# Routed experts behind a short convolution: the head laid out in a written order, with chunk 2's convolution inside

## The chip, the cores and the metric

The kernel runs on one core of a Trainium2 chip. The metric is the device time of one execution in microseconds: the median of three runs is 1276.24 us (1272.69 to 1276.6). Engines are called as in the profile: PE (TensorE matmul), PEld (its weight loads), DVE (VectorE), ACT (ScalarE), POOL (GpSimd), SP (SyncE, which only issues transfers here).

## The reference

The input x has 8 sequences of 3584 tokens with 192 channels, in fp32. Two stages are computed, one after the other:

```python
# 1. causal convolution: 8 heads of 24 channels, 7 taps, softmax of the taps
out = np.einsum('hk,bskhg->bshg', w, x_unf)
# 2. routing to one of 8 experts by cosine similarity, 1024 hidden channels
logits = (x/|x|) @ (emb/|emb|).T / tau
expert_idx = np.argmax(logits, axis=1); gate_w = softmax(logits)[expert_idx]
h = np.maximum(x[mask] @ w1[e], 0.0)
out[mask] = gate_w[mask, None] * (h @ w2[e])
```

There are 28672 tokens. Each expert has w1 (192 x 1024) and w2 (1024 x 192) in fp32, 1.5 MB together.

## The kernel before, in words

The tokens are cut into 16 chunks of 1792 (16 tiles of 112 tokens). For a chunk, `load_x` fetches its tokens into one of two buffers. `mix` does the convolution: for each of 8 heads a PE matmul in fp32 with a banded matrix (`band`, L377; two matmul records per head), an ACT copy out of PSUM (L380), then the squared norms of the tiles (L389 on ACT for 12 tiles, L392 on DVE for 4), powers of two and an inverse norm from a chain of small DVE operations (`rsqrt`, L140 to L143, then L401 to L405). `route` scales the tokens (L424 on DVE), makes fp16 high parts (L426 on ACT) and low parts (L428, L431 on DVE) in a buffer `rows` (two of them, by the chunk's parity), turns them so that channels lie on partitions, and multiplies by the experts (`logits`, L557). The rest of `route` is the ranking: softmax, the best expert, and a running count that gives every token a place `di` (L471 to L527) in a table `rows_d` in DRAM, sorted by expert. Sixteen indirect transfers per chunk, issued by POOL (L573), scatter the rows there.

An expert block is 256, 512 or 1024 tokens of one expert. `fetch` brings its rows back transposed (`e_xT`, L700, a transfer on SP's queue that waits for the scatters that it needs), `expert` does the two matmuls (L745 and L768, in split fp16), with ACT and DVE moving the hidden layer (L749, L751), and POOL scatters the result (L775). The block's expert is known only on the chip; DVE copies its weights from the image `res` into `slot` (L677, L679, L680, L683).

The experts' weights are used as fp16 high and low parts. `prep_load` brings one expert's raw weights, three transfers; `prep_weights` takes the sum of squares (a PE product, L306, whose diagonal DVE sums, L311), a power of two (L316, L151, L157, L319), three ACT operations for the high parts (L325) and three DVE operations for the low parts (L329). For experts 3 to 7 the sum of squares of w2 is an ACT operation instead (L297). Raw weights have three places: `hid`, `slot` and the end of `res`.

The head is what runs before the first expert block: constants, all eight experts' weights, chunks 0 and 1 convolved, routed and scattered. In the head the turning is done by PE (L459) with ACT copies (L463); later by transfers on SP's queue (`xtb<-rows`, 16 per chunk, L569). After chunk 1, `hand_out(2)` chooses the first seven blocks of 256 (`select`), and later hand-outs come after chunks 3, 5, 8 and 12.

What sets the order: SP's queue is in the order of the program. The other engines' queues are laid out by a scheduler in the framework with its own estimate of times; edges without a semaphore (`_dep(..., False)`) hold one instruction behind another on an engine. In the head, `HEAD` says how many steps of the chunks' work follow each step of an expert's weights, and `BEHIND` holds the work of experts 3 to 7 behind chunk 1's. After the head, `PRE` steps of the chunks' work are written ahead of the first block:

```python
PRE = 56
BEHIND = 3
HEAD = 9, 8, 9, 0, 0, 0, 0, 0
```

Then each step of a block releases some steps of the chunks' work (`dispatch`), with `TURN` steps held between the turning and the logits of a chunk.

Of the kernel before, what the change touches and what calls it, by code (L numbers as in the profile page):

```python
# [26 lines left out]
E = 8  # L27
# [42 lines left out]
class _Moe:  # L70
    def __init__(self, ctx, tc, x, weight, emb, tau, w1, w2, out):
# [35 lines left out]
        self.weights_in, self.later = False, []  # L107
# [54 lines left out]
    def constants(self):  # L162
# [20 lines left out]
        tmp = self.op.tile([128, D], F32, tag="y", name="tmp")[:, 0:2 * E].bitcast(I32)  # L183
# [9 lines left out]
        cbi = tmp[:, E:]  # L193
# [7 lines left out]
    def conv_taps(self, w):  # L201
# [19 lines left out]
        st = [self.prep_load(0)]  # L221
# [5 lines left out]
        st.append(self.prep_load(1))  # L227
        self.load_x(1)
        return st + [self.prep_load(2)]
# [54 lines left out]

    def prep_weights(self, e, st):
        nc = self.nc
# [5 lines left out]
        for k, cols in enumerate(  # L292
                ([(128, i) for i in range(NFC)] + [(64, i) for i in range(NFC, 2 * NFC)],
                 [(128, i) for i in range(2 * NFC, 2 * NFC + NFC * D // 128)])):
            if k and e >= BEHIND:

                i = nc.scalar.activation(  # L297
                    out=img[:, W2:W2 + NFC * D], in_=st[:, 2 * F:], func=AF.Square,
                    accum_out=acc[:, k:k + 1]).ins
                _dep(self.tc, i, self.act.name, False)  # L300
                yield
                continue
            tr = self.ps("h", [128, 128], F32, "tr_ps")
            for n, (rows, i) in enumerate(cols):
                v = sr[0:rows, i * 128:(i + 1) * 128]
                i = nc.tensor.matmul(out=tr, lhsT=v, rhs=v, start=(n == 0),  # L306
                                     stop=(n == len(cols) - 1)).ins
                if e >= BEHIND:
                    _dep(self.tc, i, self.turned.name, False)
            dg = self.sp.tile([128, D], F32, tag="sq", name="w_dg")[:, 0:128]  # L310
# [14 lines left out]
        hi = [nc.scalar.activation(out=o, in_=i, func=AF.Copy, scale=m).ins  # L325
              for o, i, m in ((img[:, 0:F], st[:, 0:F], s1),
                              (xb[0:64, :], st[0:64, F:2 * F], s1[0:64]),
                              (b[:, :, 0:D], s_b, s2))]
        lo = [nc.vector.scalar_tensor_tensor(  # L329
            out=o, in0=i, scalar=m, in1=h, op0=ALU.mult, op1=ALU.subtract).ins  # L330
              for o, i, m, h in (
                  (img[:, F:2 * F], st[:, 0:F], s1, img[:, 0:F]),
                  (xb[64:128, :], st[0:64, F:2 * F], s1[0:64], xb[0:64, :]),
                  (b[:, :, D:], s_b, s2, b[:, :, 0:D]))]
        self.split = lo[0]
        if e >= BEHIND:
            for i in hi:
                _dep(self.tc, i, self.act.name, False)
            for i in lo:
                _dep(self.tc, i, self.dve.name, False)  # L340
        elif e:
            for i in lo:
                _dep(self.tc, i, self.cut.name, False)
        yield


    def load_x(self, c):
# [4 lines left out]
        lo, ld = 0, []  # L352
        if r0 == 0:
            nc.gpsimd.memset(xt[0:HALO, 0, :], 0.0)
            ld = [nc.sync.dma_start(out=xt[HALO:128, 0, :], in_=xb[0:TP, :]).ins]
# [5 lines left out]
        ld.append(nc.sync.dma_start(out=xt[:, lo:, :], in_=src).ins)  # L361

        if c in self.later:
            for i in ld:
                _dep(self.tc, i, self.split.name)
# [4 lines left out]
    def mix(self, c, ring, first):  # L370
# [15 lines left out]
        for t in range(NT):  # L386
            sq = sp.tile([128, D], F32, tag="sq", name="sq")[0:TP, :]
            if t % 4 < NACT:
# [9 lines left out]
        s, si = self.pow2(n2[:], [TP, NT], 195, "x_p")  # L398
        y = self.rsqrt(n2[:], [TP, NT], "x_r")
# [7 lines left out]

        yield 1.5, 0.0
        self.mixed[c] = xc, s, si, f


    def route(self, c, xbar):
        xTs = []
        nc, sp = self.nc, self.sp
        xc, s, si, f = self.mixed.pop(c)
        r32 = self.rows2[:, c % 2]
        rows = r32.bitcast(F16)
        lg = self.ps("l", [128, NT, 2 * E], F32, "lg_ps")
        nc.vector.tensor_single_scalar(out=r32[:, :, D], in_=self.ids,
                                       scalar=float(c * CT), op=ALU.add)  # L420
        for g in range(0, NT, GX):
            u = slice(g, g + GX)
            sb = s[:, u].unsqueeze(2).to_broadcast([TP, GX, D])
            nc.vector.tensor_tensor(out=xc[:, u, :], in0=xc[:, u, :], in1=sb,  # L424
                                    op=ALU.mult)
            nc.scalar.copy(out=rows[:, u, 0:D], in_=xc[:, u, :])  # L426
            yield 0.9, 0.85
            nc.vector.tensor_tensor(  # L428
                out=rows[:, u, 256:384], in0=xc[:, u, 0:128],
                in1=rows[:, u, 0:128], op=ALU.subtract)  # L430
            self.cut = nc.vector.tensor_tensor(  # L431
                out=rows[:, u, 192:256], in0=xc[:, u, 128:192],
                in1=rows[:, u, 128:192], op=ALU.subtract).ins
            yield 0.95, 0.0

            if xbar and g < 2 * GX:
                xTs.append(self.turn(rows, g, GX))
        if c + 2 < self.nch:
            if self.weights_in:
                self.load_x(c + 2)  # L440
            else:
                self.later.append(c + 2)
        if xbar:
            for g in range(2 * GX, NT, GX):
                xTs.append(self.turn(rows, g, GX))
        if xbar:
            yield self.clock + TURN
            for g in range(NT // GX):
                self.logits(lg, xTs, g)
                yield 0.2, 0.2  # L450
                yield self.clock + GAP
        else:
            for g in range(NT // GX):
                xT = self.xt_next()
                xv = xT[:, 0:XW].rearrange("p (a k t) -> p a k t", k=3, t=TP)
                for k in range(3):
                    tp = self.ps("r", [128, GX, TP], F16, "tr_ps")
                    for a in range(GX):
                        self.turned = nc.tensor.transpose(  # L459
                            out=tp[:, a, :],  # L460
                            in_=rows[:, g * GX + a, k * 128:(k + 1) * 128],
                            identity=self.idh[:TP, :TP]).ins
                    nc.scalar.copy(out=xv[:, :, k, :], in_=tp)  # L463
                    yield 0.0, 0.5
# [419 lines left out]
    def run(self):  # L884
# [25 lines left out]
        for _ in a:  # L910
            pass
# [58 lines left out]
```

## Time and profile before

| what | value |
|---|---|
| median of the runs | 1276.24 us |
| the profiled execution: its own time, and its span | 1276.24 us, 1274.5 us |
| PE, DVE, ACT, POOL busy over the span | 89%, 66%, 46%, 43% |
| first scatter of chunk 0 starts, last scatter of chunk 1 ends | 71.68 us, 115.72 us |
| first matmul of the first block starts | 124.58 us |

The profile's times start at the beginning of the span. Busy time of an engine is the time in which at least one of its instructions ran; a row of a timeline gives start, duration, engine, line, operation, and in brackets how long the engine stood idle before it and what ended that.

### The profile page before, as it was taken

The numbers are of one execution on the slowest core, as the hardware profiler recorded it, in microseconds if no ns is written. First come the engines' busy times: TensorE is split into PE (matmuls) and PEld (weight loads), VectorE is DVE, ScalarE is ACT, GpSimd is POOL, SyncE is SP. The second block draws the span as 40 slices with busy tenths as digits, with TensorE's granted clock in tenths as the row PEclk, the third lists the DMA queues.
The fourth block names the chain that finished last, engine by engine and source line by source line (L and its number), as shares of the span: only waits on it lengthen the run. The fifth ranks groups of instructions, "written<-read, shape, count | busy, mean of one in ns | idle before, by whom it ended". The sixth has DMA issues, their size and how long they took to land.

```text
span 1274.5 us, 31268 instructions
## 1 busy us (share of the span) xinstructions
PE 1135.3 (89%) x10560; PEld 879.3 (69%) x10560; DVE 836.3 (66%) x2193; ACT 584.5 (46%) x1345; POOL 548.8 (43%) x536
## 2 busy tenths in 40 slices
PE   5543887698999999999989999999999999999998
PEld 2432666587668777666887577756777777788797
DVE  3984687598658887568696656574446545477475
ACT  3963753344545545545545453333333434333332
POOL 0055017646555745555745456474222221232222
PEclk9655989898999999999999999999999999999999
DMA  9365255664755665654536435224211122112120
GB/s 262 100 194 160 38 133 133 163 141 93 152 131 119 148 144 117 148 135 106 147 84 158 102 77 121 62 76 88 53 39 49 42 57 40 44 37 57 39 48 18
DMA packets 273432, 129.25 MB, mean 101 GB/s; under 512 B 215246, under 2 KB 263757, under 8 KB 273280
## 3 DMA queue, kind: packets, MB, share of 16 engines
q1 hardware_dynamic: 249472, 80.39, 28.4%
q0 software_dynamic: 23808, 46.87, 13.2%
q8 instruction: 91, 1.49, 0.5%
q14 instruction: 61, 0.50, 0.1%
HBM read 38.35 MB, written 47.53 MB: 67 GB/s over the span
## 4 chain that ended last, share of the span: by engine, by line
PE 40%; DVE 3%; issue 3%; POOL 2%; DMA 2%; ACT 2%; POOLq 0%; DVEq 0%; ACTq 0%; SPq 0%
PE h_ps L745 20%; PE o_ps L768 19%; DMA rows_d<-rows,di 1%; POOL rows_d L573 1%; PE conv_ps L377 1%; DVE slot L683 1%; ACT hid L749 1%; POOL out_dram L775 1%; DVE hid L751 1%; ACT sq L389 1%; DVE slot L677 0%; DMA e_xT<-rows_d 0%; DVE xt L424 0%; DVE slot L680 0%; PE lg_ps L557 0%
## 5 line engine op out<-in xcount | busy, mean ns | idle before, releaser
L768 PE MATMUL o_ps<-slot,hid 128*128 128x192 f16 x5544 | 504.2, 248 | 28.1 <-DVE slot L683 11.3
L768 PEld LDWEIGHTS <-hid 128*128 128x128 f16 x5544 | 463.2, 98 | 69.4 <-issue 19.9
L775 POOL DMA_INDIRECT out_dram<-y,e_mt x231 | 258.4, 1119 | 485.9 <-ACT y L773 449.0
L751 DVE SCALAR_TENSOR_TENSOR hid<-h_ps,hid 128x512 f16<-128x512 f32 x462 | 313.7, 686 | 146.6 <-ACT hid L749 138.8
L749 ACT ACTIVATE hid<-h_ps 128x512 f16<-128x512 f32 x462 | 271.1, 596 | 274.8 <-PE h_ps L745 263.0
L745 PE MATMUL h_ps<-e_xT,slot 128*128 128x256 f16 (+2 forms) x2592 | 343.1, 271 | 24.7 <-DMA e_xT<-rows_d 17.5
L573 POOL DMA_INDIRECT rows_d<-rows,di x256 | 273.1, 1067 | 176.4 <-issue 57.6
L745 PEld LDWEIGHTS <-slot 128*128 128x128 f16 x2592 | 222.5, 100 | 89.3 <-issue 17.0
L745 PE MATMUL h_ps<-e_xT,res 128*128 128x512 f16 x1088 | 278.8, 379 | 5.8 <-DMA e_xT<-rows_d 2.7
L773 ACT ACTIVATE y<-o_ps,g 128x192 f32<-128x192 f32 x231 | 94.2, 419 | 222.6 <-PE o_ps L768 194.9
L745 PEld LDWEIGHTS <-res 128*128 x1088 | 104.5, 98 | 126.6 <-issue 11.1
L683 DVE COPY slot<-res 128x3074 f16 x88 | 85.5, 972 | 127.1 <-PE o_ps L768 125.6
L377 PE MATMUL conv_ps<-xt,band 128*112 128x384 f32 x256 | 109.9, 525 | 19.0 <-DMA xt<-in_dram 16.0
L426 ACT CAST rows<-xt 112x768 f16<-112x768 f32 x64 | 52.9, 832 | 97.1 <-DMA rows_d<-rows,di 53.4
L380 ACT COPY xt<-conv_ps 112x384 f32<-112x384 f32 x128 | 61.1, 480 | 54.1 <-PE conv_ps L377 52.3
L389 ACT ACTIVATE sq<-xt 112x192 f32<-112x192 f32 x192 | 67.9, 355 | 4.8 <-DVE sq L392 2.7
L377 PEld LDWEIGHTS conv_ps<-xt,band 128*112 128x112 f32 x256 | 41.6, 190 | 32.7 <-issue 22.4
L677 DVE COPY slot<-res 128x3072 f16 x58 | 56.3, 971 | 4.7 <-PE h_ps L745 3.2
L424 DVE TENSOR_TENSOR xt<-xt,x_p_s 112x768 f32<-112x768 f32 x64 | 58.2, 949 | 0.1
L428 DVE TENSOR_TENSOR rows<-xt,rows 112x512 f16<-112x512 f32 x64 | 43.8, 684 | 19.1 <-ACT rows L426 17.7
L557 PEld LDWEIGHTS <-xtb 128*128 128x128 f16 x768 | 29.0, 98 | 22.9 <-DMA xtb<-rows 11.6
L557 PE MATMUL lg_ps<-ma,xtb 128*128 128x16 f16 x512 | 30.9, 171 | 15.0 <-DMA xtb<-rows 9.8
(168 smaller groups left out, 594.3 us busy)
## 6 DMA issues: line engine op xcount, KB each, us to landing
xt<-in_dram SPq DMA_DIRECT2D x8, 1536.0 KB
xt<-in_dram SPq DMA_DIRECT2D x8, 1440.0 KB
rows_d<-rows,di POOLq DMA_INDIRECT x256
out_dram<-y,e_mt POOLq DMA_INDIRECT x231
xtb<-rows SPq DMA_TRANSPOSE x224
hid<-in_dram SPq DMA_DIRECT2D x3, 768.0 KB
slot<-in_dram SPq DMA_DIRECT2D x3, 768.0 KB
hid<-in_dram SPq DMA_DIRECT2D x3, 512.0 KB
```

Source lines behind the costliest of these rows:

```text
L377: self.behind(nc.tensor.matmul(out=ps, lhsT=self.band[:, h, :], rhs=xt[:, :, h * G:(h + 1) * G], start=True, stop=True))
L380: nc.scalar.copy(out=xc[:, :, h * G:(h + 1) * G], in_=ps)
L389: nc.scalar.activation(out=sq, in_=xc[:, t, :], func=AF.Square, accum_out=n2[:, t:t + 1])
L557: i = self.nc.tensor.matmul(out=lg[:, g * GX + a, :], lhsT=xTs[g][:, u:u + 128], rhs=self.mb if k == 1 else self.ma, start=(k == 0), stop= ...
L573: i = self.nc.gpsimd.indirect_dma_start(out=self.rows_d[:, :], out_offset=bass.IndirectOffsetOnAxis(ap=idx, axis=0), in_=src, in_offset=No ...
L683: self.nc.vector.tensor_copy(out=self.slot[:, S2:], in_=self.res[:, bass.ds(self.we + W2, RES - W2)])
L745: mm = nc.tensor.matmul(out=ps[:, c, :], lhsT=w1(o, b + c), rhs=xT[:, k, :], start=(i == 0), stop=(i == 4))
L749: self.step = nc.scalar.activation(out=hh[:, b:b + m, :], in_=ps, func=AF.Relu).ins
L751: nc.vector.scalar_tensor_tensor(out=hl[:, b:b + m, :], in0=ps, scalar=0.0, in1=hh[:, b:b + m, :], op0=ALU.max, op1=ALU.subtract)
L768: mm = nc.tensor.matmul(out=o, lhsT=h[:, c, q], rhs=w2[:, c, k:k + D], start=(c + i == 0), stop=(c == NFC - 1 and i == 2))
L773: self.step = nc.scalar.activation(out=y, in_=o, func=AF.Copy, scale=g[:, a:a + 1]).ins
L775: i = nc.gpsimd.indirect_dma_start(out=self.out[:, :], out_offset=bass.IndirectOffsetOnAxis(ap=mt[:, a, 0:1], axis=0), in_=y, in_offset=No ...
```

## The change

Up to the last split of the weights, PE, DVE and ACT get one written order: a string `HEAD` of 174 characters says whose next step follows. A digit is the next step of chunk 0, 1 or 2, a letter that of expert a to h's weights. Afterwards a loop ties each instruction of PE, DVE and ACT to the one before it on its engine with an edge without a semaphore.

A chunk's generator `first` has these steps: 1 to 8 the heads of the convolution, 9 to 16 two tiles of squared norms each, 17 the powers of two; then 18 scale group 0, 19 scale 1, 20 low parts of 0, 21 scale 2, 22 low 1, 23 scale 3, 24 and 25 turn, 26 low 2, 27 and 28 turn, 29 low 3, 30 the inverse norms (`factor`), 31 to 38 turn and logits, 39 to 41 the ranking up to `di`, 42 the scatters, and for chunk 1 43 the first hand-out. Chunk 2 has only steps 1 to 17, with its inverse norms in 17. An expert's generator has 9: two sums of squares, the power of two, three high parts, three low parts.

The loads on SP's queue are: chunk 0's tokens, the band, expert a's weights, chunk 1's tokens, experts b to e, and, as places come free, chunk 2, f, g, h and chunk 3. There are five places for raw weights: three at the end of `res`, `hid` and `slot`. The sum of squares of w2 is PE's for all experts. The numbers 0 to 63 of `select` become a constant. Behind the head, `dispatch` starts with chunk 2 mixed and chunk 3 to mix, and `PRE` goes from 56 to 39.

```diff
-PRE = 56
+PRE = 39
-BEHIND = 3
-HEAD = 9, 8, 9, 0, 0, 0, 0, 0
+RAW = 2 * (2 * F + F * D // 128)
+AREAS = (2, 0), (2, 2), (2, 1), (0, 0), (1, 0), (2, 0), (0, 0), (1, 0)
+HEAD = ("0000000000000a000a00aa01101a0a011a10101aa001b111b0110110001b0b1bb1bccb"
+        "00cc0ccb0c1cc1dde100101d01dd221de20ed1ee21dd112121ee1e1211e1211222221f"
+        "f2122ff2ffffggfhh0g11ggghhghghghhh")
@@ conv_taps
-        st = [self.prep_load(0)]
         self.band = cp.tile([128, H, TP], F32, name="band")
...
-        st.append(self.prep_load(1))
-        self.load_x(1)
-        return st + [self.prep_load(2)]
@@ prep_load
-        st = (self.hid[:], self.slot[:], self.res[:, (E - 2) * RES:])[e % 3].bitcast(F32)[:, 0:2 * F + NFC * D]
+        k, n = AREAS[e]
+        at = E * RES - (n + 1) * RAW if k == 2 else 0
+        st = (self.hid, self.slot, self.res)[k][:, at:at + RAW].bitcast(F32)
@@ prep_weights
-            if k and e >= BEHIND:
-                i = nc.scalar.activation(
-                    out=img[:, W2:W2 + NFC * D], in_=st[:, 2 * F:], func=AF.Square,
-                    accum_out=acc[:, k:k + 1]).ins
...
+        for o, i, m in ((img[:, 0:F], st[:, 0:F], s1),
+                        (xb[0:64, :], st[0:64, F:2 * F], s1[0:64]),
+                        (b[:, :, 0:D], s_b, s2)):
+            nc.scalar.activation(out=o, in_=i, func=AF.Copy, scale=m)
+            yield
...
@@ mix
-            sq = sp.tile([128, D], F32, tag="sq", name="sq")[0:TP, :]
+            sq = self.lp.tile([128, D], F32, tag="sqa" if act else "sqv", name="sq")[0:TP, :]
@@ new: first
+    def first(self, c):
+        nc = self.nc
+        yield from self.mix(c, "h")
+        if c >= PICK[0]:
+            return
+        rows = self.rows2[:, c % 2].bitcast(F16)
+        f = lg = None
+        steps = [(self.scaled, 0), (self.scaled, 1), (self.rest, 0), (self.scaled, 2),
+                 (self.rest, 1), (self.scaled, 3), 0, 1, (self.rest, 2), 2, 3,
+                 (self.rest, 3), None, 4, 5, 6, 7, 8, 9, 10, 11]
...
+        yield from self.rank(c, lg, f)
@@ dispatch
+        last, cb, ca = self.nch, PICK[0], PICK[0] + 1
@@ run
-        st = self.conv_taps(w)
+        self.conv_taps(w)
+        st = [self.prep_load(0)]
+        self.load_x(1)
+        st += [self.prep_load(e) for e in range(1, 5)]
         self.embeddings(em, tb)
...
+        work = {"012"[c]: self.first(c) for c in range(PICK[0] + 1)}
+        work.update({"abcdefgh"[e]: self.prep_weights(e, st) for e in range(E)})
+        load = lambda e: lambda: st.append(self.prep_load(e))
+        wait = [("0", 29, lambda: self.load_x(2)), ("a", 9, load(5)),
+                ("d", 9, load(6)), ("e", 9, load(7)), ("1", 29, lambda: self.load_x(3))]
+        done = dict.fromkeys(work, 0)
+        for k in HEAD:
+            next(work[k])
+            done[k] += 1
+            while wait and done[wait[0][0]] >= wait[0][1]:
+                wait.pop(0)[2]()
...
+        end = {}
+        for i in self.nc.cur_bb.bb.instructions[at:]:
+            if i.engine in (self.nc.tensor.engine, self.nc.vector.engine,
+                            self.nc.scalar.engine):
+                if i.engine in end:
+                    _dep(self.tc, i, end[i.engine].name, False)
+                end[i.engine] = i
+        self.mm = end[self.nc.tensor.engine].name
         while self.ready < min(3, len(self.subs)):
             self.fetch()
-        a = self.dispatch(first, "r")
+        a = self.dispatch()
```

The ranking (`rank`) and the halves of a group (`scaled`, `rest`, `factor`) are the code of `route` and `mix` before, cut into functions.

## Rows read from the trace of the kernel before

**Rows 1.** Busy us by stage (x instructions), granted PE clock, DMA share, GB/s

```profile
45.00:71.70 26.70, 15.00 (x196) 12.01 (x195) 24.85 (x82) 22.11 (x44) 0.06 (x2) 0.50 0.40 119
71.70:110.00 38.30, 10.67 (x79) 8.57 (x76) 30.04 (x87) 25.80 (x26) 30.07 (x28) 0.50 0.49 151
110.00:124.60 14.60, 5.67 (x11) 2.63 (x12) 3.38 (x5) 2.40 (x5) 5.87 (x6) 0.62 0.83 254
```

**Rows 2.** Timeline, end of the head: places, scatters, fetch, first block

```profile
71.68 1.10 POOL L573 DMA_INDIRECT rows_d<-rows,di  x1 [26.64 <-DVE di L527]
...
79.27 0.15 DVE L527 TENSOR_SCALAR di<-dr 112x16 int32<-112x16 f32 x1
79.32 0.94 POOL L573 DMA_INDIRECT rows_d<-rows,di  x1 [0.30 <-issue]
...
109.93 2.05 POOL L573 DMA_INDIRECT rows_d<-rows,di  x1 [0.31 <-issue]
110.91 0.95 DVE L677 COPY slot<-res 128x3072 f16 x1
...
114.78 0.94 POOL L573 DMA_INDIRECT rows_d<-rows,di  x1 [0.30 <-issue]
...
121.34 1.33 SPq L700 DMA_TRANSPOSE e_xT<-rows_d  x1
...
124.58 4.00 PE L745 MATMUL h_ps<-e_xT,slot 128*128 128x256 f16 x18 [3.40 <-DMA e_xT<-rows_d]
...
127.11 1.31 SPq L700 DMA_TRANSPOSE e_xT<-rows_d  x1
```

**Rows 3.** Timeline, begin of the head: the band's load and the first convolution

```profile
9.62 0.38 SPq L224 DMA_DIRECT2D band<-cseq_d  x1
...
16.63 7.54 PE L377 MATMUL conv_ps<-xt,band 128*112 128x384 f32 x16 [2.79 <-issue]
```

**Rows 4.** DVE by line and shape, 0 to 124 us: busy us, mean ns

```profile
L424 DVE TENSOR_TENSOR xt<-xt,x_p_s 112x768 f32<-112x768 f32 x8 | 7.3, 948 | 0.0
L329 DVE SCALAR_TENSOR_TENSOR res<-hid,w_p_s,res 128x1536 f16<-128x1536 f32 x3 | 5.4, 1811 | 0.0
L428 DVE TENSOR_TENSOR rows<-xt,rows 112x512 f16<-112x512 f32 x8 | 5.4, 679 | 0.0
L329 DVE SCALAR_TENSOR_TENSOR res<-hid,w_p_s,res 128x1024 f16<-128x1024 f32 x3 | 3.8, 1277 | 0.7 <-ACT res L325 0.7
L431 DVE TENSOR_TENSOR rows<-xt,rows 112x256 f16<-112x256 f32 x8 | 3.3, 412 | 0.0
L311 DVE SCALAR_TENSOR_TENSOR w_dg<-tr_ps,idf 128x128 f32<-128x128 f32 x11 | 3.1, 285 | 18.9 <-ACT sq L389 11.0 <-PE tr_ps L306 7.6
L141 DVE SCALAR_TENSOR_TENSOR x_r_t<-x_r_t,n 112x16 f32<-112x16 f32 x6 | 1.0, 170 | 0.1
```

**Rows 5.** Chain that ended last: one step, the landing of a scatter

```profile
611.77 2.46 DMA rows_d<-rows,di
```

**Rows 6.** PE by line, 124.5 to 150 us

```profile
L377 PE MATMUL conv_ps<-xt,band 128*112 128x384 f32 x22 | 9.7, 522 | 0.0
```

**Rows 7.** Waits of PE, 124 to 260 us: total, times, longest

```profile
PE h_ps L745 <- DMA e_xT<-rows_d: 17.5, 4, 10.6
PE lg_ps L557 <- DMA xtb<-rows: 9.8, 10, 2.1
```

**Rows 8.** Timeline after the head: chunk 2's turning, scatters, eighth fetch, a later wait

```profile
146.78 10.82 SPq L569 DMA_TRANSPOSE xtb<-rows  x8
...
158.74 13.10 SPq L569 DMA_TRANSPOSE xtb<-rows  x8
...
189.48 1.55 POOL L573 DMA_INDIRECT rows_d<-rows,di  x1 [15.40 <-DVE sl_ai L613]
...
218.84 2.41 SPq L700 DMA_TRANSPOSE e_xT<-rows_d  x1
...
251.51 2.31 PE L745 MATMUL h_ps<-e_xT,slot 128*128 128x256 f16 x10 [10.56 <-DMA e_xT<-rows_d]
```

More of the change, by code (lines that the diff above doesn't have):

```diff
@@ L191, in constants @@
         nc.gpsimd.memset(self.rst[:, :, 0:1], 0.0)
-        cbi = tmp[:, E:]
+        nums = tmp[0:1, E:E + 64]
+        nc.gpsimd.iota(nums, pattern=[[1, 64]], base=0, channel_multiplier=0)
+        self.nums = cp.tile([1, 64], F32, name="nums")
+        nc.vector.tensor_copy(out=self.nums, in_=nums)
+        cbi = tmp[:, E + 64:]
         nc.gpsimd.iota(cbi, pattern=[[self.cap, E]], base=0, channel_multiplier=0)
@@ L305, in prep_weights @@
                 v = sr[0:rows, i * 128:(i + 1) * 128]
[L306 to L310, printed above, removed]
+                nc.tensor.matmul(out=tr, lhsT=v, rhs=v, start=(n == 0),
+                                 stop=(n == len(cols) - 1))
+            dg = self.lp.tile([128, D], F32, tag="sqv", name="w_dg")[:, 0:128]
             nc.vector.scalar_tensor_tensor(
@@ L360, in load_x, with mix @@
             ap=[[D, 128], [TP * D, NT - lo], [1, D]])
[L361 to L365, printed above, removed]
+        nc.sync.dma_start(out=xt[:, lo:, :], in_=src)
         self.xts.append(xt)
-    def mix(self, c, ring, first):
+    def mix(self, c, ring):
         nc, sp = self.nc, self.sp
@@ L406, in mix @@
                                 scalar2=None, op0=ALU.mult)
-        yield 1.5, 0.0
-        self.mixed[c] = xc, s, si, f
-    def route(self, c, xbar):
-        xTs = []
-        nc, sp = self.nc, self.sp
[L415 to L464, printed above, removed]
-                xTs.append(xT)
-                self.logits(lg, xTs, g)
-                yield 0.2, 0.2
@@ new lines, in factor, with scaled, rest @@
+        return f
+    def scaled(self, c, g):
+        xc, s = self.mixed[c][:2]
+        u = slice(g * GX, g * GX + GX)
+        sb = s[:, u].unsqueeze(2).to_broadcast([TP, GX, D])
+        self.nc.vector.tensor_tensor(out=xc[:, u, :], in0=xc[:, u, :], in1=sb,
+                                     op=ALU.mult)
+        self.nc.scalar.copy(out=self.rows2[:, c % 2].bitcast(F16)[:, u, 0:D],
+                            in_=xc[:, u, :])
+    def rest(self, c, g):
+        xc, u = self.mixed[c][0], slice(g * GX, g * GX + GX)
+        rows = self.rows2[:, c % 2].bitcast(F16)
+        self.nc.vector.tensor_tensor(
+            out=rows[:, u, 256:384], in0=xc[:, u, 0:128],
+            in1=rows[:, u, 0:128], op=ALU.subtract)
+        self.nc.vector.tensor_tensor(
+            out=rows[:, u, 192:256], in0=xc[:, u, 128:192],
+            in1=rows[:, u, 128:192], op=ALU.subtract)
@@ new lines, in route @@
+    def route(self, c):
+        xTs = []
+        lg = self.ps("l", [128, NT, 2 * E], F32, "lg_ps")
+        for g in range(NT // GX):
+            self.scaled(c, g)
+            yield 0.9, 0.85
+            self.rest(c, g)
+            yield 0.95, 0.0
+            if g < 2:
+                xTs.append(self.turn(c, g))
+        if c + 2 < self.nch:
+            self.load_x(c + 2)
+        for g in range(2, NT // GX):
+            xTs.append(self.turn(c, g))
+        yield self.clock + TURN
+        for g in range(NT // GX):
+            self.logits(lg, xTs[g], g)
+            yield 0.2, 0.2
+            yield self.clock + GAP
+        yield from self.rank(c, lg, self.mixed[c][4])
@@ L479, in route @@
         ex = sp.tile([TP, NT, E], F32, tag="ea", name="ex")
-        self.act = nc.scalar.activation(out=ex, in_=l, func=AF.Exp).ins
+        nc.scalar.activation(out=ex, in_=l, func=AF.Exp)
+        if head:
+            yield
         z = sp.tile([TP, NT], F32, tag="z", name="z")
@@ L505, in route @@
         yield 2.5, 0.2
-        if xbar:
+        if not head:
             yield self.clock + RANK
@@ L533, in route @@
             self.hand_out(c + 1)
-        while self.pend and not xbar:
-            self.put()
-            yield 0.15, 0.15
+        if head:
+            while self.pend:
+                self.put()
+            yield
+        if c + 1 == PICK[0]:
+            self.hand_out(c + 1)
+            yield
     def put(self, step=None):
```

138 lines of the change are left out of this document (70 added, 68 removed).

## The prediction

> **What bounds the kernel now.** I read the page, then the stretches, then the timeline of the head's end, then the waits of PE behind it. Up to 110 us the head belongs to DVE: 24.85 of 26.7 us busy from 45 to 71.7, 30.04 of 38.3 from 71.7 to 110, while PE has 15.0 and 10.67 [rows 1]. From 110 to 124.6 nothing computes much (DVE 3.38, ACT 2.40 of 14.6). What ends last is a chain on POOL: the scatters start at 71.68, when chunk 0's places are ready, and end at 114.78 + 0.94 = 115.72, the first fetch is issued at 121.34, the first matmul of a block starts at 124.58 [rows 2]. So 32 scatters took 44.04 us, 1.376 each. Chunk 1's places came at 79.27 + 0.15 = 79.42 [rows 2], when POOL still had some ten scatters of chunk 0 to do, so they never made POOL wait.
>
> Behind the head PE does not simply run. From 124 to 260 us it waits 17.5 us for a block's rows and 9.8 for turned tokens [rows 7]. The reason is SP's queue: chunk 2 is loaded, convolved and cut late, so its turning starts at 146.78, and its 16 transfers hold the queue to 158.74 + 13.10 = 171.84, with the fetches of later blocks behind them; its scatters start at 189.48 and the eighth fetch, the first that needs them, is issued at 218.84 [rows 8]. One wait of 10.56 us stands later, at 251.51 [rows 8]. The profiled execution has the median's time, 1276.24 us, its span 1274.5; sums below are against it.
>
> **The change: begin of the head.** The band's load is issued at 9.62, after the taps have landed, and the first convolution starts at 16.63 and takes 7.54 [rows 3]. In the band's queue stood expert a's 1.5 MB; now only chunk 0's tokens do. At least nothing is won, at most the band lands as a scatter does, 2.46 us [rows 5] after 9.62 + 0.38, and the start moves by 16.63 - 12.46 = 4.2. I take 3.9, near the upper end, since what stood ahead is gone: start 12.7, end 20.2, copies and first DVE work at 21.2. Five places for raw weights are worth nothing by themselves while DVE is the bound; they cover against late loads. The constant that replaces an iota and a cast per selection is under 1 us.
>
> **DVE's written list.** Costs from [rows 4], busy over count: scaling a group 7.3/8 = 0.91; low parts of a group (5.4 + 3.3)/8 = 1.09; low parts of an expert 5.4/3 = 1.8 for w2 and 3.8/3 = 1.27 for each of the two parts of w1, 4.35; a sum of squares 3.1/11 = 0.28, for which I take 0.36 with the read-out of its sum; a tile's norm on DVE, 192 columns where L311 has 128, 0.285 x 1.5 = 0.43. Small operations that wait for the one before take 0.17 and a gap, 0.2 (0.15 for those in the power of two of weights). A ranking is some 13 operations of 0.28 (like the 128x128 of L311), 8 small ones and one ACT operation: 5.5.
> Up to chunk 0's places the list holds chunk 0's steps to 41, chunk 1's to 24, experts a to c, d to its third step, e's first. That is 8 scalings 7.3, 6 low parts 6.5, 8 norms 3.4, one inverse norm of 16 small 3.2, 6 small 1.2, a ranking 5.5, three experts' low parts 13.0, 9 sums of squares 3.2, 4 powers of two 2.4: together 45.7. With 2.4 for the wait on ACT's squares of chunk 0 the places are there at 21.2 + 45.7 + 2.4 = 69.3 (before 71.7).
> From there to chunk 1's places: 2 low parts 2.2, inverse norm 3.2, ranking 5.5, experts d and e 8.7, 3 norms of chunk 2 1.3, 3 sums of squares 1.1, a power of two 0.6: 22.6, so 91.9 (before 79.4: chunk 1 is later by 12.5, which was hidden behind POOL).
> To the end: selection 23 small 4.6, rest of chunk 2 4.2, experts f to h 13.0, 4 sums 1.4, 3 powers 1.8, 1.5 for waits: 26.5, so 118.4. Then DVE copies the first block's w1 to slot (0.95 for L677 [rows 2], and two halves that I put at the same together): 120.3.
> The five sums of squares of w2 that leave ACT are among the DVE terms; ACT's list is shorter than DVE's in either version (22.11 against 24.85, 25.80 against 30.04 [rows 1]), so what ACT saves counts nothing. PE has room for the added products.
>
> **POOL's chain.** First 16 scatters from 69.7 to 91.7; chunk 1's places are there at 91.9, just no longer in time; second 16 to 92.3 + 22.0 = 114.3. Landing 2.46 [rows 5] (before 121.34 - 115.72 = 5.6, with the loads of chunks 2 and 3 moving 254 GB/s in 110 to 124.6 [rows 1]; these now come earlier): fetch at 116.8. From fetch to matmul 124.58 - 121.34 = 3.24: first block at 120.0, beside DVE's 120.3. So the first block gains only 4.3 us: 124.58 to 120.3.
>
> **What moves behind the head.** In 124.5 to 150 PE spent 9.7 us on 22 convolution records, six of chunk 2 and 16 of chunk 3 [rows 6]. Chunk 2's are now in the head, and chunk 3's can run while PE's list is done and the scatters still go. The larger term is SP's queue. Chunk 2 needs only scaling and low parts, 4 x (0.91 + 1.09) = 8 us on DVE, the first group within 2; so its turning stands right behind the first three fetches. The third was issued 127.11 - 121.34 = 5.8 after the first [rows 2], with 1.7 more for itself: 120.3 - 3.24 + 5.8 + 1.7 = 124.5, against 146.78, 22.3 us earlier. All that followed it on SP to the eighth fetch was the queue itself or the chain through ranking and scatters, and moves along: 218.84 to 196.5. Is PE then in time? Until the eighth fetch lands at 218.84 + 3.24 = 222.1 it lost 17.5 + 9.8 - 10.56 = 16.7 us to waits, so its work from 124.6 was some 222.1 - 124.6 - 16.7 = 81, now 81 - 9.7 = 71: from 120.3 to 191.5, when SP's chain brings the eighth block's rows at 199.8. SP decides, and 22.3 of it come out. The wait at 251.51 comes from the same queue (16 transfers of chunk 4) and stays. 1276.2 - 22.3 = 1254.
>
> **The rivals.** (B) The list is slower. The granted clock was 0.50 of full, 1.2 GHz, from 45 to 110 us, with PE busy 15.0 of 26.7 [rows 1]; were it so from the first convolution on, and each turn and sum of squares in a strict order passed from engine to engine at that rate, I put 7 us on the first block (the 2.4 of waits above, again in each of three stretches): turning at 131.5, 15.3 earlier, 1261. By the Trainium skill (TensorE: Matmul & The Clock Gate, Part 1: The HAM clock gate) the throttled rate is the default and activity lifts it, which speaks against a head that spreads PE's work thin; the trace agrees, with its 0.50.
> (C) SP's head start is not used: steps of ranking and scatters are released by the blocks' progress on PE, so chunk 2's rows are asked for as late as before, counted in blocks. Then only the first block's 4.3 and chunk 2's six records (6/22 of 9.7 = 2.6) are left: 1269. For it: turning and logits are written a fixed number of steps apart. Against it: the eighth fetch followed the last scatters, and these went back to back from 189.48.
> (D) Slower: the scatters. All 32 now run beside a full DVE, and the longest took 2.05, while DVE copied to slot at its end [rows 2]; with the gap of 0.30 that is 2.35 each, 75.2 for 32. From 69.7 they would end at 144.9, the first block would start at 150.6, the turning at 154.8, 8 later than 146.78: 1284. It decides from 2.1 us per scatter. Against it: the one at 79.32 took 0.94 [rows 2], in a stretch with DVE busy 30.04 of 38.3 us [rows 1]. By the Trainium skill (SBUF — State Buffer, Who interferes with whom) VectorE and GpSimd share a pair of ports that one holds for a whole instruction, among others for copies; the row of 2.05 that ends with the copy L677 agrees.
> (E) More: the waits that I leave also go, because everything on SP stands further ahead, 10.56 more: 1243.
>
> **How the numbers follow.** Chances: forecast (A) 0.42, B 0.18, C 0.15, D 0.13, E 0.12. Time 1254. Range 1238 to 1278: it holds A, B, C and E with 2 to 5 us around, leaves out D and a small rest below. 0.3% is 3.8 us, about what can be told from no change. Faster: A 0.41, B 0.16, C 0.11, E 0.11, together 0.79; within: 0.07, from the weak ends of A, B, C and E; slower: D and 0.01 of C, 0.14.
>
> **What would show it.** Right: first convolution near 13 us, places of chunk 0 near 69 and of chunk 1 near 92, no gap on POOL between the halves, first block near 120, chunk 2's turning near 125, eighth fetch near 197. B shows as both places late, C as an eighth fetch that moves less than the turning, D as scatters over 2 us, E as a small wait where 10.56 stood. Wrong at the root: DVE with long idle stretches before 110, or a first block after 143.

## The result, and the profile after

The changed kernel takes 1264.66 us in the median of four runs (1262.08 to 1266.82), the kernel before 1276.05 beside it: ratio 0.9915, 95% interval 0.989 to 0.9941. That is faster by 11.4 us, or 10.8 by the ratio, about half of the 22.3 forecast; the time lies inside the range and 10.7 us above the predicted 1254. The profiled execution took 1265.17 us, its span is 1263.5.

The stretches of the head, as in [rows 1], for the changed kernel (busy us and instructions of PE, PEld, DVE, ACT, POOL, granted clock, DMA share, GB/s):

```profile
45.00:71.70 26.70, 18.67 (x183) 14.60 (x183) 24.53 (x73) 21.46 (x35) 0.65 (x1) 0.66 0.43 119
71.70:110.00 38.30, 15.54 (x180) 11.46 (x176) 31.97 (x95) 21.78 (x49) 30.08 (x28) 0.74 0.62 190
110.00:124.60 14.60, 6.81 (x12) 3.06 (x12) 7.59 (x41) 5.93 (x7) 5.73 (x6) 0.50 0.15 42
```

PE is busy longer in the first two, at a higher clock (0.66 and 0.74, means of the two levels 0.50 and 1.00, where 0.50 stood). In the third nobody is busy for long, as before, though DVE still has experts' weights to split. The timeline of the same time, beside [rows 2] and [rows 3]:

```profile
14.00 4.78 PE L361 MATMUL conv_ps<-xt,band 128*112 128x384 f32 x7 [5.62 <-DMA band<-cseq_d]
...
70.58 0.17 DVE L550 TENSOR_SCALAR di<-dr 112x16 int32<-112x16 f32 x1
71.05 1.10 POOL L599 DMA_INDIRECT rows_d<-rows,di  x1 [27.61 <-DVE w_p_s L159]
...
91.39 0.17 DVE L550 TENSOR_SCALAR di<-dr 112x16 int32<-112x16 f32 x1
91.87 0.94 POOL L599 DMA_INDIRECT rows_d<-rows,di  x1 [0.30 <-issue]
...
97.44 0.33 DVE L507 TENSOR_SCALAR rows<-ids 112x16 int32<-112x16 int32 x1 [4.62 <-DMA rows_d<-rows,di]
...
115.77 0.94 POOL L599 DMA_INDIRECT rows_d<-rows,di  x1 [0.30 <-issue]
118.72 0.18 DVE L507 TENSOR_SCALAR rows<-ids 112x16 int32<-112x16 int32 x1 [4.95 <-DMA rows_d<-rows,di]
...
122.55 1.33 SPq L724 DMA_TRANSPOSE e_xT<-rows_d  x1
...
128.04 4.44 DVE L329 SCALAR_TENSOR_TENSOR res<-slot,w_p_s,res 128x1024 f16<-128x1024 f32 x3
...
135.50 1.01 PE L769 MATMUL h_ps<-e_xT,slot 128*128 128x256 f16 x4
```

Up to 92 us all is near the forecast: places of chunk 0 at 70.75 (69.3 forecast), of chunk 1 at 91.56 (91.9), no gap on POOL, 32 scatters from 71.05 to 116.71, 1.43 us each (1.376 before). Then DVE goes out of the forecast. At 97.44 and 118.72 L507 writes the token numbers of chunks 2 and 3 into row buffers that the scatters of chunks 0 and 1 still read, so it waits for their landing: 4.62 and 4.95 us. It was to come with the ranking of those chunks, far behind the head; the scheduler, which has only to keep the written order of the head's own instructions, put it between them. It put chunk 2's cut there too (four scalings, 3.64 us, and eight low parts, 4.37, from 97.58 on). The list's last split ends at 132.48, where I had 118.4; the first block starts at 135.5, where I had 120.3 and where 124.58 stood before.

SP's queue behind the head, beside [rows 8], and two waits of PE from 124 to 260 us, beside [rows 7]:

```profile
130.40 10.31 SPq L595 DMA_TRANSPOSE xtb<-rows  x8
...
141.85 13.20 SPq L595 DMA_TRANSPOSE xtb<-rows  x8
...
172.49 1.32 POOL L599 DMA_INDIRECT rows_d<-rows,di  x1 [0.31 <-DVE sl_av L641]
...
200.70 1.24 SPq L724 DMA_TRANSPOSE e_xT<-rows_d  x1
```

```profile
PE h_ps L769 <- DMA e_xT<-rows_d: 11.0, 2, 6.4
...
PE lg_ps L583 <- DMA xtb<-rows: 4.8, 6, 1.1
```

Chunk 2's turning starts 16.4 us earlier than before (22.3 forecast), its scatters 17.0, the eighth fetch 18.1. The first fetch was late by 122.55 - 116.8 = 5.75 against the forecast, and the turning stands 7.85 behind it, near the forecast's 7.5.

To see what became of it I sum PE's busy time backwards from the end, in windows of 10 us, and read at what time so much of it was left. PE has the same work in both (1135.3 and 1135.4 us busy), so a difference in time at one mark is idle time saved or lost up to there. Differences to the kernel before, in us; the kernels e9 to e16 are those of the experiments. Their busy time is 1133.7 to 1144.0, so a few us of a difference can be busy time there.

```
                  first    turning  eighth  | 910 us   700     610     10    | median
                  block    starts   fetch   | left     left    left    left  | of the runs
before            124.58   146.78   218.84  | at 326.9 544.7   638.8   1259.4| 1276.05
changed           135.50   130.40   200.70  | -15.9    -14.4    -9.2   -10.9 | 1264.66
e16 (the same)    134.83   129.73   200.02  | -17.1    -15.5   -11.2   -11.4 | 1263.75
e13 ids           130.99   125.80   195.33  | -20.5    -18.7   -15.8   -18.0 | 1257.79
e14 ids, logits   125.79   125.40   197.42  | -18.3    -12.6   -15.6   -18.1 | 1258.12
e15 cut, logits   125.94   129.13   199.99  | -12.3     -7.1   -10.2   -10.9 | 1262.99
e9  all three     121.95   125.45   198.84  | -18.8    -13.9   -16.8   -20.7 | 1255.61
e10 turn first    131.00   101.87   196.44  | -21.2    -17.3   -11.9   -12.4 | 1262.17
e11 lower rate    135.77   130.67   201.49  | -13.3    -10.1    -7.3    -6.8 | 1269.82
e12 turn first,   132.65   103.45   197.49  | -18.5    -11.6    -6.0   -10.9 | 1264.35
    higher rate
```

At the mark of 910 us left the change is ahead by 15.9, nearly what the turning's start gained (16.4); by 610 it has given 6.7 of it back, and from there to the end it wins 1.7. So two things are missing: 5.9 us of head start, and 5 that were won and lost again.

### The profile page after: what moved, and what is told of

It reads as the page before. It is cut to its first block, busy times and chain, and to the rows that moved or that the text cites. A ratio compares the mean times of both kernels' runs of the same rounds, so it can differ in the third digit from the quotient of the medians.

```text
span 1263.5 us, 31371 instructions
## 1 busy us (share of the span) xinstructions
PE 1135.4 (90%) x10620; PEld 880.0 (70%) x10620; DVE 844.0 (67%) x2192; ACT 584.1 (46%) x1335; POOL 552.5 (44%) x525
## 3 DMA queue, kind: packets, MB, share of 16 engines
q0 software_dynamic: 23808, 46.87, 13.3%
## 4 chain that ended last, share of the span: by engine, by line
PE 42%; issue 4%; DMA 3%; DVE 2%; POOL 2%; ACT 1%; POOLq 0%; DVEq 0%; ACTq 0%
PE h_ps L769 20%; PE o_ps L792 20%; DMA rows_d<-rows,di 2%; POOL rows_d L599 1%; DVE slot L707 1%; PE conv_ps L361 1%; POOL out_dram L799 1%; DVE hid L775 1%; ACT hid L773 0%; DVE slot L701 0%; DMA e_xT<-rows_d 0%; PE lg_ps L583 0%; DMA out_dram<-y,e_mt 0%; DVE slot L704 0%; DMA xtb<-rows 0%
## 5 line engine op out<-in xcount | busy, mean ns | idle before, releaser
L769 PE MATMUL h_ps<-e_xT,slot 128*128 128x256 f16 (+2 forms) x2592 | 335.9, 269 | 17.6 <-DMA e_xT<-rows_d 11.0
L599 POOL DMA_INDIRECT rows_d<-rows,di x256 | 279.9, 1093 | 162.3 <-ACT hid L773 58.1
L361 PE MATMUL conv_ps<-xt,band 128*112 128x384 f32 x256 | 114.4, 546 | 16.8 <-ACT xt L364 10.2
L419 DVE TENSOR_TENSOR rows<-xt,rows 112x512 f16<-112x512 f32 x64 | 43.8, 684 | 18.7 <-ACT rows L412 18.1
L704 DVE COPY slot<-res 64x1024 f16 x88 | 39.9, 454 | 1.5
```

The costliest lines, as they stand in the source:

```text
L361: self.behind(nc.tensor.matmul(out=ps, lhsT=self.band[:, h, :], rhs=xt[:, :, h * G:(h + 1) * G], start=True, stop=True))
L599: i = self.nc.gpsimd.indirect_dma_start(out=self.rows_d[:, :], out_offset=bass.IndirectOffsetOnAxis(ap=idx, axis=0), in_=src, in_offset=No ...
L769: mm = nc.tensor.matmul(out=ps[:, c, :], lhsT=w1(o, b + c), rhs=xT[:, k, :], start=(i == 0), stop=(i == 4))
```

## Experiments

The theories: S, the start of chunk 2's turning on SP's queue decides (the prediction's); F, the first block's start decides; later P and Q, on what is given back; W, L and C are told in the expectations that use them. Ratios are to the kernel before on the same chip. The chips were of two kinds: with before near 1276 us (e9 to e16), and with before at 1372 to 1406 (e1 to e8, e17, e18), where engines wait for nothing that the profile shows; the last section has the rows. Reasons are read from the first kind, and those runs come first.

**e16, the change again.** 

> The changed kernel on the chip of this call: 0.9915 of before (0.989 to 0.994) if the chip is like that of e9 to e12, first block at 135.5, turning at 130.4; the others are read against it.

Measured: 1263.75 (1260.23 to 1269.04), ratio 0.9905 (0.9876 to 0.9934).

**e13, token numbers held behind their own ranking.**

```diff
-        nc.vector.tensor_single_scalar(out=r32[:, :, D], in_=self.ids,
-                                       scalar=float(c * CT), op=ALU.add)
+        ids = nc.vector.tensor_single_scalar(out=r32[:, :, D], in_=self.ids,
+                                             scalar=float(c * CT), op=ALU.add).ins
+        if not head:
+            _dep(self.tc, ids, first.name, False)
```

(`first` is the ranking's first reduction.) 

> e1 once more: the token numbers of later chunks held behind their own ranking, nothing else. Theory W (the waits on the scatters' landing decide): the selection 4 us earlier, first fetch at 119 to 120, turning at 127 to 128, time 3 to 6 us below the changed kernel. Theory L (the first block stands behind chunk 2's logits in TensorE's order): first block still at 133 to 135, time within 2 us of the changed kernel (it was 0.997 of it on the slower chips).

Measured: 1257.79 (1253.38 to 1260.01), ratio 0.985 (0.9796 to 0.9904): 6.0 below e16, on the same chip, with no run of one among those of the other. Its timeline: first fetch, the list's last split, turning, first block:

```profile
117.97 1.33 SPq L726 DMA_TRANSPOSE e_xT<-rows_d  x1
...
118.56 4.44 DVE L329 SCALAR_TENSOR_TENSOR res<-slot,w_p_s,res 128x1024 f16<-128x1024 f32 x3
...
125.80 10.40 SPq L597 DMA_TRANSPOSE xtb<-rows  x8
...
130.99 3.58 PE L771 MATMUL h_ps<-e_xT,slot 128*128 128x256 f16 x16
```

Without the two waits the first fetch is issued 3.9 us earlier than in e16, and the turning with it; the list ends at 123.00, 9.5 before the change's. Theory W holds, with the turning 1 to 2 us earlier than it said.

**e14, the same, and chunk 2's logits later in PE's order.** The cut stays ahead of the last splits.

```diff
-        yield self.clock + TURN
+        yield self.clock + (TURN if c > PICK[0] else 32.0)
```

> Token numbers held and chunk 2's logits 32 steps behind its turning, but its cut left where the scheduler puts it (7.5 us of VectorE ahead of the last splits). Theory L: first block at 128 to 132, time 3 to 6 us below the changed kernel. Theory C (the cut in VectorE's list is what counts): within 2 us of the changed kernel.

Measured: 1258.12 (1257.21 to 1258.38), ratio 0.9858 (0.9809 to 0.9907).

```profile
117.58 1.33 SPq L726 DMA_TRANSPOSE e_xT<-rows_d  x1
...
125.40 10.31 SPq L597 DMA_TRANSPOSE xtb<-rows  x8
...
125.79 6.03 PE L771 MATMUL h_ps<-e_xT,slot 128*128 128x256 f16 x40 [2.48 <-DVE slot L703]
```

The first block starts 5.2 us earlier than in e13, where chunk 2's logits stood ahead of it and waited for turned tokens, the longest time 5.13 us. The turning starts at nearly the same time (0.4 earlier), and the time is e13's. What the expectation put down to the first block (L) is e13's gain; the block's start by itself brought nothing, and theory C, which had the time of the change, fell.

**e15, cut and logits held, token numbers left.**

```diff
+        if c == PICK[0]:
+            _dep(self.tc, i, self.head_dve, False)
```

(`i` is the scaling of a group, `head_dve` the last instruction of DVE's written list; with e14's edit.) 

> Chunk 2's cut and logits held as in e9, but the token numbers left where they are, with their two waits on landings (9.6 us). Theory W: first block at 131 to 135 and the time of the changed kernel within 3 us. Theory C: first block at 124 to 128 and 6 to 10 us below the changed kernel.

Measured: 1262.99 (1262.17 to 1265.3), ratio 0.9895 (0.9846 to 0.9944): e16's time.

```profile
97.24 0.36 DVE L509 TENSOR_SCALAR rows<-ids 112x16 int32<-112x16 int32 x1 [4.60 <-DMA rows_d<-rows,di]
...
115.85 1.33 SPq L726 DMA_TRANSPOSE e_xT<-rows_d  x1
...
125.94 6.60 PE L771 MATMUL h_ps<-e_xT,slot 128*128 128x256 f16 x40 [6.61 <-DVE slot L703]
...
129.13 10.89 SPq L597 DMA_TRANSPOSE xtb<-rows  x8
```

Here the first block starts 8.9 us earlier than in e16 and the turning, which now waits for the late cut, 0.6: no gain. The first fetch is issued 6.0 us earlier too (121.89 in e16), so it is not the first fetch by itself either. With e14 this speaks against F from both sides. (Theory W had the first block at 131 to 135; one of the two waits, 4.60, was left in the list. Theory C had the block right and the time wrong.)

**e9, all three holds.** 

> The changed kernel with three holds: the token numbers of later chunks behind their own ranking (as e1), chunk 2's cut on VectorE behind the head's last split, and chunk 2's logits 32 steps after its turning and not 14, so that they stand behind the first blocks in TensorE's order. The first block should then start at 124 to 127 us (135.5 in the change), while the turning still stands behind the first three fetches and starts at 128 to 132. Theory F (the first block decides): 8 to 11 us below the changed kernel. Theory S (the start of chunk 2's turning decides): within 2 us of the changed kernel.

Measured: 1255.61 (1254.42 to 1256.03), ratio 0.9847 (0.98 to 0.9893), the fastest. Its timeline, the list's last split first:

```profile
112.54 4.44 DVE L329 SCALAR_TENSOR_TENSOR res<-slot,w_p_s,res 128x1024 f16<-128x1024 f32 x3
...
117.62 1.33 SPq L728 DMA_TRANSPOSE e_xT<-rows_d  x1
...
121.95 5.87 PE L773 MATMUL h_ps<-e_xT,slot 128*128 128x256 f16 x40 [5.68 <-DVE slot L705]
125.45 10.89 SPq L599 DMA_TRANSPOSE xtb<-rows  x8
```

It is 9.1 below the changed kernel (of another chip; 8.7 by the ratios), as F said. But I had not seen that the turning would start 5 us earlier too, so this run alone did not tell F from S; e13 to e15 do. It is also the forecast's head: fetch 117.62 (116.8 forecast), first block 121.95 (120.3), turning 125.45 (124.5), time 1255.61 (1254).

**e10, the turning ahead of the first three fetches** in SP's order (the loop of fetches moved behind the loop over PRE). 

> e4 once more, beside the others of this call: the first three fetches stand behind chunk 2's turning on SyncE's queue, so that the turning starts at 103.5 and the first block at 133. Theory S: 10 to 15 us below the changed kernel (some of the 27 us of head start cannot be used, since TensorE then has no wait left: in e4 it was 12 us by equal TensorE work). Rival (e4's gain belonged to its chip): within 2 us of the changed kernel.

Measured: 1262.17 (1258.84 to 1264.25), ratio 0.9897 (0.9866 to 0.9928). 28.5 us of head start, and 2.5 us of gain, so S's 10 to 15 fell. The table shows where most of it went: the eighth fetch is only 4.3 us earlier than in the change. Chunk 2's scatters start 12.8 earlier, at 159.67, and take 32.4 us to the end of the sixteenth at 192.05, where the change took 23.8 (172.49 to 196.25). The marks show the rest: at 910 us left e10 is 5.3 ahead of the change, at 610 still 2.7, and 9.3 of its 21.2 are given back between.

**e11, a lower rate of preparation,** and **e12, a higher one on e10.** The account of preparation done (`spent`) sets how much of later chunks is put between two steps of an expert; before, it began with chunk 2's convolution in it.

```diff
-        spent = [0.0, 0.0]
+        spent = [2.58, 7.88]
```

> e7 once more: the account of preparation started at 2.58 and 7.88 us, so a lower rate of preparation between the experts' steps. Theory P (the higher rate of the change gives back 5 us between 410 and 640 us): 3 to 6 us below the changed kernel. Rival Q (preparation that comes earlier is what the later blocks wait for; on the other chip the lower rate cost 11 us): 3 to 15 us above it.

> e10 with the account of preparation started below zero by the same 2.58 and 7.88 us, so a higher rate than the change's. Rival Q: 2 to 10 us below e10. Theory P: 3 to 6 us above e10.

Measured: e11 1269.82 (1266.52 to 1272.29), ratio 0.9964 (0.9943 to 0.9985); e12 (minus the same) 1264.35 (1260.92 to 1268.69), 0.9904 (0.9874 to 0.9933). Neither theory holds whole. From 910 to 610 us left e11 gives back 6.0 and e12 12.5, against 6.7 of the change and 9.3 of e10: the sign is P's. But e11 is behind already at 910 (-13.3), and its sum is a loss, as Q said; and the faster rate gains nothing.

**What is given back, in rows.** The stretch from 700 to 610 us of PE's work left, by windows, first before, then the change, then e9:

```profile
544.70:638.80 94.10, 89.97 (x800) 67.07 (x798) 67.06 (x217) 49.19 (x129) 58.97 (x59) 0.98 0.52 130
```

```profile
530.30:629.50 99.20, 90.34 (x795) 67.19 (x792) 65.33 (x189) 50.04 (x126) 60.44 (x57) 0.98 0.50 123
```

```profile
530.80:621.90 91.10, 90.09 (x832) 68.65 (x830) 63.74 (x200) 48.59 (x118) 57.45 (x55) 1.00 0.61 132
```

PE needs 90 us for it in all three, and idles 4.1, 8.9 and 1.0. Its waits there, in the change and in e9 (total, times, longest):

```profile
PE o_ps L792 <- ACT hid L773: 4.0, 2, 2.8
PE o_ps L792 <- DVE hid L775: 2.0, 2, 1.5
PE h_ps L769 <- DVE hid L775: 1.7, 2, 1.1
```

```profile
PE o_ps L796 <- DVE hid L779: 0.6, 1, 0.6
PE h_ps L773 <- DVE hid L779: 0.4, 1, 0.4
```

PE waits for the two halves of an expert's hidden values, which ACT and DVE make. Neither is full in the stretch (DVE 65.33, ACT 50.04 of 99.20). What stands ahead of the hidden values in two of the change's waits:

```profile
563.65 0.83 ACT L412 CAST rows<-xt 112x768 f16<-112x768 f32 x1 [4.99 <-DMA rows_d<-rows,di]
564.39 1.56 ACT L773 ACTIVATE hid<-h_ps 128x512 f16<-128x512 f32 x3
565.04 3.71 PE L792 MATMUL o_ps<-slot,hid 128*128 128x192 f16 x39 [1.14 <-ACT hid L773]
...
601.99 0.18 DVE L507 TENSOR_SCALAR rows<-ids 112x16 int32<-112x16 int32 x1 [3.49 <-DMA rows_d<-rows,di]
602.70 0.69 DVE L775 SCALAR_TENSOR_TENSOR hid<-h_ps,hid 128x512 f16<-128x512 f32 x1 [0.52 <-DVE rows L507]
603.45 1.33 PE L792 MATMUL o_ps<-slot,hid 128*128 128x192 f16 x14 [1.45 <-DVE hid L775]
```

It is the head's wait again: a later chunk's write into `rows` waits for scatters to land, and the hidden values stand behind it in the engine's order. In this stretch ACT waits so for 14.3 us in the change, 10.5 in before and 7.7 in e9, in the order of PE's idle time (8.9, 4.1 and 1.0). No run takes these waits away alone, so this is read from rows and not shown.

The three kernels with late logits (e9, e14, e15) give back 2.0 to 2.7 us from 910 to 610, the others 4.7 to 12.5, so the logits' place may be part of it. (Against before, e9 loses 4.9 from 910 to 700 and wins 2.9 of it back in the stretch above.) What else sets it I leave open.

**On the slower chips.** e1, e4 and e6 are e13, e10 and e17 there, e7 is e11, e5 the change. e2 leaves chunk 2's convolution out of the head, e3 is the kernel before with one edit; e8 is e6 with `PRE` 24:

```diff
-            if self.weights_in:
-                self.load_x(c + 2)
-            else:
-                self.later.append(c + 2)
+            self.load_x(c + 2)
```

> The changed kernel, with one edge more: writing the token numbers of a chunk behind the head into its rows is held behind the first operation of that chunk's ranking on DVE. In the changed kernel DVE stood idle before that write for 4.62 us at 92.8 and 4.95 us at 113.8, until scatters had landed, with the last three experts' splits and the choice of the blocks queued behind it. So the first block should start some 9 us earlier (126 instead of 135.5) and the first fetch at 119 instead of 122.55. Theory S (SP's queue decides: the time follows the start of chunk 2's turning, 130.4): the turning moves 3.6 earlier, 1261. Theory F (the first block decides): 1255 to 1256. If the waits of DVE are covered by something else: 1264.

> The changed kernel without chunk 2 in the written order: its 17 steps go back behind the head (56 steps ahead of the first block, as before), all else as changed, chunk 2's load early too. DVE's list in the head is 4 us shorter. Theory S: chunk 2's turning starts when its convolution and cut are done after the head, about 138 to 142 instead of 130.4, and the time is 8 to 12 us longer: 1273 to 1277. If the written order and the early loads make the gain and not the convolution inside: 1262 to 1266.

> The kernel before, with one part of the change alone: chunks 2 and 3 are loaded as soon as their buffers are free instead of behind the last split. PE is idle before the first block from 103 to 124 us, so chunk 2's convolution can run there. Theory S: turning starts earlier than 146.8 by 10 us or more, 1262 to 1268. If it takes the written order to bring chunk 2's work forward: 1274 to 1277, with turning near 145.

> The changed kernel with SP's queue reordered: the first three fetches are written behind chunk 2's turning instead of ahead of it. SP was idle from 85.5 to 122.5 and chunk 2's rows were cut by 105.2. Turning should start near 103 instead of 130.4 and end near 128, the first fetch near 129 instead of 122.55, the first block as before at 135 (DVE's list ends at 132.5). Theory S: the eighth fetch moves by 15 us or more and the time by 6 to 15: 1250 to 1258. Theory F: 1264 to 1267.

Measured, before at 1388.17: e1 1344.33 (ratio 0.9646 to 0.972), e2 1384.6 (0.9931 to 0.9985), e3 1377.87 (0.9859 to 0.9944), e4 1336.31 (0.9587 to 0.9668).

> The changed kernel once more, on the chip of this call, so that the other three kernels have it beside them. Where the chip runs like the first one, 0.9915 of before is expected (0.989 to 0.994) with a first block at 135.5 us. Where it runs like the chip of e1 to e4 (before at 1388 us): theory F (the two waits on scatter landings in VectorE's list, 9.57 us, cost what they last) puts it 9 us above e1, about 0.975 of before; theory S (SyncE's start of chunk 2's turning decides, and e1's stood at 130.01 against 130.40 of the change) puts it at e1's ratio, 0.968 within 0.004.

> e1 and e4 together: the token numbers of later chunks held behind their own ranking, and the first three fetches behind chunk 2's turning in SyncE's order. Theory S: turning starts near 103.5 as in e4, and the time is e4's or up to 3 us below it (0.960 to 0.965 of before on e4's chip; 26 us below the changed kernel if every us of SyncE's head start counts). Theory F: the first block decides; it stood at 132.8 in e4 and 135.2 in e1, because SyncE's 16 turns now stand ahead of the first fetch, so the gain over the changed kernel is 3 us or less.

> The changed kernel, with the account of preparation already done started at chunk 2's convolution and norms (2.58 us of VectorE, 7.88 us of ScalarE), as it stood before the change, where that work was done after the head; so the rate at which preparation is put between the experts' steps goes back toward before's. Theory P (the 7 us given back between the 33rd and the 99th output come from a higher rate that makes TensorE wait): 4 to 7 us below the changed kernel. Rival (they come from SyncE's and GpSimd's work lying elsewhere, whatever the rate): within 1.5 us of the changed kernel.

> e6 with 24 steps of preparation ahead of the first block in place of 39, so that chunk 2's logits stand behind the first experts' matmuls in TensorE's order and not ahead of them. Theory L (the first block in e1 waits in TensorE's order for the logits, which wait 9.1 us for turned rows): first block 2 to 6 us earlier than in e6 and the time lower by as much. Rival (the later preparation is short in the same measure afterwards): within 2 us of e6, and the 8th fetch no earlier.

Measured, the ratios against two runs of before at 1362.76 and 1381.91 (its others took up to 1395.94): e5 1347.52 (0.9694 to 0.9938), e6 1341.4 (0.9656 to 0.9893), e7 1358.81 (0.977 to 1.0042), e8 1368.71 (0.9846 to 1.0096).

> e6 once more, on the chip of this call: token numbers held and the turning first on SyncE's queue. If the gain of an earlier turning is used up at about 5 us of head start (what e10 showed), 0.982 to 0.988 of before, no better than e13's 0.985. If e10's small gain came from the two waits of token numbers that it still had, 0.97 to 0.98.

> e9 once more, beside e17 on one chip: 0.9847 of before (0.980 to 0.989), with a first block at 122 us and the turning at 125.5.

Measured, before at 1405.9: e17 1353.7 (0.9595 to 0.9659), e18, which is e9, 1371.41 (0.974 to 0.9803).

There the turning ahead of the fetches is best: e17 is 18 us below e18, e6 6 below e5 and e4 8 below e1, each pair on one chip, while e10 stands above e13 (0.9897 against 0.985, on two chips). The kernel of e6 and e17 was not run on the first kind of chip. e1 is 3 us below e5, on another chip, where e13 gained 6. Without chunk 2's convolution in the head (e2, turning at 142.41) nearly the whole gain is gone. The early loads alone (e3, turning at 142.38) bring 0.9902, about half of e5's gain within wide intervals; whether they would on the first kind of chip was not tested. The sign of "preparation earlier is better" agrees (e7 is 11 us above e5 and e8 27 above e6, as e11 is slower), its size does not carry over, and none of the expectations for e6, e7, e8, e17 and e18 was met. And e6 and e17, one kernel, stand at 0.9775 and 0.9627 on two such chips, so a per cent between chips of this kind tells nothing.

## Where the prediction was right and where it failed

**The head up to 92 us: right.** First convolution at 14.00 (12.7), places within 1.5 us, POOL without a gap. The scatters took 1.43 each: D, which needed 2.1, is out; the longest took 2.17 (at 110.82), beside low parts of an expert (L329, 1.81 at 110.36) and no copy to `slot`; half of the 2.05 of before lay beside such low parts too (L329, 109.17 to 110.99), ahead of the copy that the prediction names.

**The written list's end: wrong, and the step that failed.** "To the end: ... 26.5, so 118.4" counted the head's own instructions and took the list for closed. It ended at 132.48. The runs take the 14.1 us of difference apart: without L507's two waits (9.57) the list ends at 123.00 (e13), 9.5 earlier; without chunk 2's cut too (which I priced at 8 us, but behind the list) at 116.98 (e9), 6.0 earlier again; so the 118.4 was 1.4 too much for what it counted. I named no wait for L507, though the diff shows that it is moved, and that its buffer is the scatters' source. The trace of before had the sign, a wait that cost little there, since of the head's list only a copy stood behind it:

```profile
121.32 0.18 DVE L419 TENSOR_SCALAR rows<-ids 112x16 int32<-112x16 int32 x1 [9.00 <-DMA rows_d<-rows,di]
121.45 0.97 DVE L683 COPY slot<-res 128x3074 f16 x1
```

e13 takes the two waits away and gets 6.0 us.

**SP decides: right in the mechanism for this change.** The turning stands 7.85 behind the first fetch in the change, 7.83 in e13 and e9, near the forecast's 7.5; the first block alone brings nothing (e14, e15); at 910 us left the change is ahead by nearly what the turning gained. The term was mis-sized, 16.4 for 22.3. But that the chain to the eighth fetch "moves along" is no rule: in e10 the turning moves 28.5 and the eighth fetch 4.3. What a kernel is ahead of before at 910 us left follows the eighth fetch, 1.2 to 4.1 us short of what that moved (6.6 in e15); no run moves it alone. That the first block, 10.9 later than before, cost nothing I would not have guessed.

**"22.3 of it come out": wrong in a second place.** I carried the head start to the end unpaid. 5.2 of it are lost from 700 to 610 us left, with PE waiting 4.0, 2.0 and 1.7 for ACT and DVE. e9, with nearly the forecast's head, idles 1.0 there and ends 1.6 above the forecast; it too gives back 2.0 from 910 to 610.

**The rivals.** B had the nearest numbers (turning 131.5, 1261), by another cause: the clock in the head was 0.66 and 0.74, not 0.50, and the places were in time; the list was late by waits for landings. By the Trainium skill (TensorE: Matmul & The Clock Gate, Part 1: The HAM clock gate) activity lifts the rate. The trace agrees in the first two stretches, with PE busy 18.67 and 15.54 where it had 15.00 and 10.67 [rows 1]; in the third it does not show it, with 6.81 at 0.50 where 5.67 stood at 0.62. C is out for this change: the eighth fetch moved 18.1, more than the turning; e10 shows what C described. E is half there: where a wait of 10.56 stood [rows 8] one of 4.63 stands, at 232.37.

## What to carry to other kernels

An order written by hand holds only among the instructions that are in it: look what else the scheduler may put between them, above all a write into a buffer that a transfer still reads, since it stops the whole engine until the landing. When an early start is to be carried to the end, count the idle time at equal work left; here a head start of the turning paid nearly in full where the eighth fetch moved with it (the change), and hardly where it did not (e10). Where waits for a landing come back later, look for the writes behind which other work stands. Two versions within a per cent of each other can change places on another chip, as e1 and e4 did against e13 and e10.

## What the hardware showed

By the start of the write that waits for it, a scatter's landing took 2.01 us behind the last one (116.71 to 118.72, DMA at 59 GB/s from 100 to 117 us) and 4.63 behind the sixteenth (92.81 to 97.44, 285 GB/s from 85 to 93); in e16 2.01 and 6.49.

The same kernel took 1264 us on some chips and 1348 on another (e5). Of the 84.4 us between the two profiled spans, 35 are longer busy time of PE (1170.4 against 1135.4, at a granted clock of 0.94 and 0.96), the rest is idle time. The waits of PE for which the profile names no releaser, in e5 and, below, in the change:

```profile
PE o_ps L792 <- issue: 51.4, 58, 2.5
...
PE lg_ps L583 <- issue: 13.3, 17, 1.4
```

```profile
PE h_ps L769 <- issue: 0.6, 2, 0.3
```

In all they are 75.3 us in 96 waits against 0.6 in 2. Read at the same output blocks, e5 falls behind until about 880 us of the change's trace, some 85 us by then, and hardly further to the end. What the engines wait for the profile does not show.
